# Linear attention and a split-precision MLP: larger units of k features, other burst prices in the planner, other SBUF addresses

## The chip, the cores and the metric

The kernel runs on one core of a Trainium2 chip. The metric is the time of one execution in microseconds (us) of device time. Three runs of the kernel before took 1173.62 to 1175.29 us, median 1174.64. The chip's engines are called as in the profile: PE is TensorE (matmuls; PEld is its weight load), DVE is VectorE, ACT is ScalarE, POOL is GpSimd, SP is SyncE, which only issues DMAs here.

## The reference

```python
def _attn_ref(q, k, v, w_phi):              # q, k, v: 8 batches, 8 heads, 576 tokens, 64; w_phi: 64 x 128
    def phi(x):
        proj = np.einsum('bhsd,df->bhsf', x, w_phi)
        proj = proj - np.max(np.abs(proj), axis=-1, keepdims=True)
        return np.concatenate([np.exp(proj), np.exp(-proj)], axis=-1)
    q_p, k_p = (phi(q), phi(k))
    kv = np.einsum('bhsf,bhsd->bhfd', k_p, v)
    z = np.sum(k_p, axis=2)
    num = np.einsum('bhsf,bhfd->bhsd', q_p, kv)
    den = np.einsum('bhsf,bhf->bhs', q_p, z)[..., None] + 1e-06
    return (num / den).astype(np.float32)

def _moe_ref(x, w_in, w_out):               # x: the attention's output as 4608 x 512
    h = x @ w_in                            # 512 x 2048
    g = 0.5 * h * (1.0 + erf(h * inv_sqrt2))
    return (g @ w_out).astype(np.float32)   # 2048 x 512
```

## The kernel before

There are two streams of work on one TensorE. The attention stream handles 8 batches one after another. For each batch there are two quads of four heads (`k_quad`): a projection `pk` of the keys, its largest absolute value per token (`mx`, DVE, L412), the difference (DVE, through the helper at L328), two exps to `ek` (ACT, L416), and the sums `kv` over tokens (PE), which ACT copies to `kvn`. A quad's nine chunks of 128 tokens are taken in five units of 2, 2, 1, 2 and 2 chunks. Then come the query halves (`q_pair`): a projection `pq`, a copy `pc` to SBUF, an all-reduce `mb` of absolute values over the partitions on POOL (L459), the difference (DVE, L328), two exps `ef` (ACT, L465), and the numerator `pn` (PE). The denominator comes from TensorE in batches 0 and 1, and later from DVE (`un`, L488 and L491) and a second POOL all-reduce (`db`, L494). Numerator and denominator go to DRAM (`x_d`, `d_d`); `quotients` inverts the denominators.

The MLP stream has 18 blocks of 256 tokens (`block`). A block reads its tokens back (`xr`, `rb`), multiplies them on DVE and splits the product into a high part `xh` and a low part `xl`. Eight units follow. In each, 24 matmuls of 128x256 (`ph`) are followed by gelu on ACT (`gh`, L581 and L582), the low part `gl` on DVE (L328), and 12 matmuls of 128x512 (`po`). A block has 192 `ph` and 96 `po` matmuls; three matmuls (high by high, high by low, low by high) make one product. The weights arrive as 64-bit floats in 32 tiles (`w_i`, `w_o`), and each is converted and split by two operations on ACT and five on DVE (`split_weight`, L343 to L350).

No engine's order is written by hand. Every operation is given to a planner (class `Plan`) with an engine, a cost in us, a rank and a kind. `order` walks through time: on each engine it takes, among the operations that can go, the one of lowest rank; attention on TensorE is held back during the MLP until a lump of it (`LUMP`) has gathered. A change of tile shape on TensorE costs what `BEHIND` and `BEFORE` say. The engines then run their queues in that order. `T0`, `AT`, `ATR`, `HOLD`, `EARLY` and `WPACE` set when batches, blocks and weights come due. An operation cannot start before its tile's slot is free: one slot for `pk` and `pq` together (`pp`), one for `pn`, two for `ph`, one for `po`, four for `ek`, two for `gh` and `gl`.

SBUF tiles are allocated in the order of the `place` calls. Built, this kernel has `w_o8` to `w_o15` at addresses that are 0x700 past a multiple of 0x1000 (0x13700 and so on), `w_o0` to `w_o7` at 0x7c0 past one (0x1b7c0 and so on), and both slots of `xh` and `xl` at 0x7c0 past one.

All matmuls are recorded under one helper line, L287. An fp32 matmul (`pk`, `kv`, `pq`, `pn`) is one instruction in the program and two records in the trace; `ph` and `po` have one.

Of the kernel before, what the change touches and what calls it, by code (L numbers as in the profile page):

```python
# [54 lines left out]
class Op:  # L55
    __slots__ = ("eng", "cost", "fn", "bufs", "rank", "table", "late", "deps", "users", "wait", "ready", "start", "end", "n", "names", "nbytes", "duty", "kind")


class Plan:
# [45 lines left out]
    def order(self, bias):  # L105
# [53 lines left out]
        while len(done) < n:  # L159
# [79 lines left out]
def mm_cost(m, n):  # L239
    return max(0.875 * m, n / 2.306 + 9) / 1e3  # L240
# [27 lines left out]
def fused_kernel(ctx: ExitStack, tc: tile.TileContext, qT, kT, va, w_st, w_in, w_out, out):  # L268
# [11 lines left out]
    SLOTS = dict(kt=2, vt=2, mx=2, ek=4, kvn=4, un=1, db=1, qt=2, pc=2, mb=1, ef=2, xo=2, dc=2, rb=1, xr=1, xh=2, xl=2, gh=2, gl=2, ob=2)  # L280
# [100 lines left out]
    def k_quad(b, g, kvs, rank):  # L381
# [17 lines left out]
        units = ((0, (0, 1)), (0, (2, 3)), (None, (4,)), (1, (5, 6)), (1, (7, 8)))  # L399
        for u, (p, cs) in enumerate(units):  # L400
            n = len(cs)
            mx = sb["mx"]([P, 2, n], F32, f"mx_{nm}_{u}")
            e = [sb["ek"]([P, 2, n, NF], F32, f"ek_{nm}_{u}_{s}") for s in range(2)]
# [3 lines left out]
            def proj(x=x, cs=cs):  # L407
# [3 lines left out]
            op("pe", n * PAIR_K, proj, r=[kt, wst], w=[x], also=[mx, *e], kind="k", **k())  # L411
            op("dve", dve(256 * n, True), lambda xs=xs, mx=mx: nc.vector.tensor_reduce(  # L412
                out=mx(), in_=xs(), axis=AX.X, op=ALU.max, apply_absolute_value=True), r=[x], w=[mx], **k())
            tt("dve", dve(256 * n, True), xs, xs, lambda mx=mx, n=n: mx().unsqueeze(3).to_broadcast([P, 2, n, NF]), ALU.subtract, [x, mx], [x], **k())
            for s in (1, 0):
                op("act", act(256 * n, True), lambda xs=xs, e=e, s=s: nc.scalar.activation(  # L416
                    e[s](), xs(), AF.Exp, scale=1.0 - 2.0 * s), r=[x], w=[e[s]], table="exp", **k())
            for pp in (0, 1) if p is None else (p,):
# [5 lines left out]
                last_u = (u == 2) if pp == 0 else (u == 4)  # L424
                for i, c in enumerate(cs):
# [11 lines left out]
                    op("pe", 4 * PAIR_V, sums, r=[*e, vt] + ([] if fresh and i == 0 else [acc]), w=[acc], kind="v", **k())  # L437
# [4 lines left out]
    def q_pair(b, p, kvs, rank, halves=(0, 1)):  # L442
# [4 lines left out]
        for half in halves:  # L447
# [12 lines left out]
                mb(), pc(), P, bass_isa.ReduceOp.absmax), r=[pc], w=[mb], **k(1))  # L460
# [33 lines left out]
            op("pool", 3.7, lambda db=db, un=un: nc.gpsimd.partition_all_reduce(db(), un(), P, bass_isa.ReduceOp.add), r=[un], w=[db], **k())  # L494
# [43 lines left out]
    def block(j, rank):  # L538
# [22 lines left out]
        copy("dve", dve(NCC * TB, fast=True), xh, xr, [xr], [xh], rank=rank(0) - 4)  # L561
        tt("dve", dve(NCC * TB), xl, xr, lambda: xh().bitcast(F32), ALU.subtract, [xr, xh], [xl], rank=rank(0) - 4)
        po = ps["po"]([P, 2, DM], F32, f"po_{j}")
        for u in range(NU):
            rk = rank(u / NU)
            ph = ps["ph"]([P, 2, TB], F32, f"ph_{j}_{u}")
            for i in range(2):
# [10 lines left out]
                op("pe", 12 * mm_cost(128, TB), mm1, r=[xh, xl] + [wi[c, u // 2] for c in range(NCC)], w=[ph], rank=rk)  # L578
# [112 lines left out]
```

## Time and profile before

| | |
|---|---|
| median of 3 runs | 1174.64 us (1173.62 to 1175.29) |
| profiled execution | 1172.59 us |
| its span in the trace | 1170.8 us, 21787 instructions |
| mean granted TensorE clock | 0.981 of full speed |
| busy: PE, PEld, DVE, ACT, POOL | 95%, 78%, 42%, 50%, 27% of the span |
| chain that ended last | PE 79%, DVE 7%, DMA 4%, ACT 3%, POOL 3% |
| first matmul of blocks 0, 1, 2, 10 and 17 | 94.1, 171.5, 255.9, 808.8, 1121.4 us |

The span runs from the first to the last recorded instruction; the profiled execution's time is 1.8 us longer, and the median of the timed runs is another 2.05 us above that. The share of busy time is a mean over stages with different limits, so the stages are shown apart below. The page shows the span in 40 slices of 29.3 us, a digit being tenths of a slice; its PE row reads 5679999989 in the first ten slices and 9 in nearly all after them. Block 10's first matmul is the last before which attention is still under way; the eight blocks after it follow each other every 44 us.

### The profile page before, as it was taken

The page shows a single profiled execution, that of the slowest core. Times are in us where ns is not written, and L with a number is a line of the kernel's source. Part 1 is how long each engine was busy: PE and PEld are TensorE (multiplying, and loading weights), DVE is VectorE, ACT ScalarE, POOL GpSimd, SP SyncE. Part 2 cuts the span into 40 slices and gives each one's busy share as a digit, 9 for nine tenths or more (in the row PEclk, how much of TensorE's full clock was granted, in tenths as well). Part 3 has the DMA queues.
Part 4 walks back from the last instruction along what each step waited for, and adds up shares of the span by engine and source line. Part 5 has one row for each costly group of instructions (what it writes and reads, how often), then busy time and mean ns, then how long its engine had stood idle before and what let it go on. Part 6 is the DMA issues. An engine that isn't in the chain of part 4 may idle for free.

```text
span 1170.8 us, 21787 instructions
## 1 busy us (share of the span) xinstructions
PE 1116.8 (95%) x9096; PEld 917.1 (78%) x9096; DVE 486.6 (42%) x807; ACT 589.7 (50%) x963; POOL 320.7 (27%) x116
## 2 busy tenths in 40 slices
PE   5679999989899999999999999999999999999998
PEld 3437688767778778787877877787989989899897
DVE  5899942365553634444343444425121121121110
ACT  4676755745565676667466666755122122122121
POOL 3120200355561734445263454516000000000000
PEclk8799999989999999999999999999999999999999
DMA  6567421133322141322113130211121011010000
GB/s 240 177 210 228 139 71 47 52 94 102 94 65 70 41 107 45 108 64 80 58 43 106 43 106 23 69 28 51 27 55 36 19 54 37 18 37 19 1 18 19
DMA packets 73940, 84.92 MB, mean 73 GB/s; under 512 B 23969, under 2 KB 60993, under 8 KB 73841
## 3 DMA queue, kind: packets, MB, share of 16 engines
q1 hardware_dynamic: 73840, 83.52, 23.9%
q8 instruction: 71, 1.16, 0.4%
q14 instruction: 29, 0.23, 0.1%
HBM read 64.32 MB, written 19.17 MB: 71 GB/s over the span
## 4 chain that ended last, share of the span: by engine, by line
PE 79%; DVE 7%; DMA 4%; ACT 3%; POOL 3%; issue 2%; SPq 1%; ACTq 0%; POOLq 0%; DVEq 0%
PE po L287 32%; PE ph L287 31%; PE kv L287 6%; PE pn L287 5%; PE pq L287 3%; PE pk L287 3%; POOL db L494 2%; DMA raw_i<-in_w_in_dram 1%; DMA x_d<-xo 1%; POOL mb L459 1%; DVE pc L328 1%; DMA dc<-d_d 1%; ACT ek L416 1%; DVE w_o L328 1%; DVE w_i L328 0%
## 5 line engine op out<-in xcount | busy, mean ns | idle before, releaser
L287 PE MATMUL ph<-xh,w_i 128*128 128x256 f32 x2304 | 431.3, 283 | 0.0
L287 PEld LDWEIGHTS ph<-xh,w_i 128*128 128x128 f32 x2304 | 363.0, 190 | 15.4 <-issue 6.5
L287 PE MATMUL po<-w_o,gh 128*128 128x512 f32 x1152 | 367.6, 400 | 1.1 <-ACT gh L581 1.0
L287 PE MATMUL ph<-xl,w_i 128*128 128x256 f32 x1152 | 322.3, 280 | 0.0
L287 PEld LDWEIGHTS po<-w_o,gh 128*128 128x128 f32 x1152 | 208.6, 189 | 56.1 <-issue 8.2
L328 DVE TENSOR_TENSOR gl<-ph,gh 128x512 fp32r<-128x512 f32 x144 | 99.0, 688 | 361.7 <-ACT ph L582 353.0
L459 POOL PARTITION_ALL_REDUCE mb<-pc x64 | 144.6, 2259 | 362.4 <-ACT pc L322 327.7
L287 PE MATMUL po<-w_o,gl 128*128 128x512 f32 x576 | 228.8, 397 | 7.2 <-DVE gl L328 7.1
L287 PEld LDWEIGHTS ph<-xl,w_i 128*128 128x128 f32 x1152 | 218.4, 190 | 3.1
L581 ACT ACTIVATE gh<-ph 128x512 fp32r<-128x512 f32 x144 | 86.1, 598 | 259.2 <-PE ph L287 258.5
L494 POOL PARTITION_ALL_REDUCE db<-un x48 | 177.1, 3690 | 134.3 <-DVE un L491 119.3
L287 PEld LDWEIGHTS po<-w_o,gl 128*128 128x128 f32 x576 | 108.7, 189 | 36.4 <-DVE gl L328 11.9
L287 PEld LDWEIGHTS kv<-vt,ek 128*64 128x64 f32 (+1 forms) x2560 | 87.8, 143 | 43.1 <-ACT ek L416 18.1
L287 PE MATMUL kv<-vt,ek 128*64 128x65 f32 (+1 forms) x2560 | 99.8, 231 | 15.7 <-ACT ek L416 14.7
L287 PE MATMUL pn<-ef,kvn 128*64 128x288 f32 (+1 forms) x512 | 97.7, 427 | 16.1 <-ACT xo L322 11.1
L416 ACT ACTIVATE ek<-pk 128x512 f32<-128x512 f32 (+1 forms) x160 | 80.0, 550 | 46.3 <-DVE pk L328 45.9
L465 ACT ACTIVATE ef<-pc 128x576 f32<-128x576 f32 x128 | 81.7, 679 | 30.5 <-DVE pc L328 30.2
L328 DVE TENSOR_TENSOR pc<-pc,mb 128x576 f32<-128x576 f32 x64 | 55.1, 861 | 100.0 <-POOL mb L459 99.7
L412 DVE TENSOR_REDUCE mx<-pk 128x4 f32<-128x512 f32 (+1 forms) x80 | 50.4, 632 | 90.2 <-PE pk L287 90.2
L582 ACT ACTIVATE ph<-ph 128x512 f32<-128x512 f32 x144 | 85.4, 593 | 0.0
L581 ACT ACT_TABLE_LOAD x55 | 70.6, 1283 | 19.8 <-PE ph L287 19.1
L287 PEld LDWEIGHTS pn<-ef,kvn 128*64 128x64 f32 (+1 forms) x512 | 39.4, 138 | 52.2 <-ACT xo L322 19.3
(41 smaller groups left out, 697.4 us busy)
## 6 DMA issues: line engine op xcount, KB each, us to landing
vt<-in_va_dram SPq DMA_DIRECT2D x16, 585.0 KB
qt<-in_qT_dram SPq DMA_DIRECT2D x64, 144.0 KB
kt<-in_kT_dram SPq DMA_DIRECT2D x16, 576.0 KB
out_dram<-ob SPq DMA_DIRECT2D x36, 256.0 KB
raw_i<-in_w_in_dram SPq DMA_DIRECT2D x16, 512.0 KB
raw_o<-in_w_out_dram SPq DMA_DIRECT2D x16, 512.0 KB
x_d<-xo SPq DMA_DIRECT2D x48, 144.0 KB
x_d<-xo SPq DMA_DIRECT2D x32, 72.0 KB
```

The costliest lines, as they stand in the source:

```text
L287: return tc.keep_in_program_order(nc.tensor.matmul(*a, **kw))
L328: op(eng, cost, lambda: e.tensor_tensor(out=dst(), in0=a(), in1=b(), op=o), r=r, w=w, **kw)
L412: op("dve", dve(256 * n, True), lambda xs=xs, mx=mx: nc.vector.tensor_reduce(out=mx(), in_=xs(), axis=AX.X, op=ALU.max, apply_absolute_val ...
L416: op("act", act(256 * n, True), lambda xs=xs, e=e, s=s: nc.scalar.activation(e[s](), xs(), AF.Exp, scale=1.0 - 2.0 * s), r=[x], w=[e[s]], ...
L459: op("pool", 2.2, lambda mb=mb, pc=pc: nc.gpsimd.partition_all_reduce(mb(), pc(), P, bass_isa.ReduceOp.absmax), r=[pc], w=[mb], **k(1))
L465: op("act", act(2 * HS), lambda ef=ef, pc=pc, s=s: nc.scalar.activation(ef()[:, s], pc(), AF.Exp, scale=1.0 - 2.0 * s), r=[pc], w=[ef], ta ...
L494: op("pool", 3.7, lambda db=db, un=un: nc.gpsimd.partition_all_reduce(db(), un(), P, bass_isa.ReduceOp.add), r=[un], w=[db], **k())
L581: op("act", act(2 * TB, True) + 0.016, lambda gh=gh, ph=ph: nc.scalar.activation(gh(), ph(), AF.Gelu), r=[ph], w=[gh], table="gelu", rank= ...
L582: op("act", act(2 * TB, True) + 0.037, lambda ph=ph: nc.scalar.activation(ph(), ph(), AF.Gelu), r=[ph], w=[ph], table="gelu", rank=URGE + rk)
```

## The change

The k units become three per quad, of 4, 1 and 4 chunks. The subtraction writes its difference to the SBUF tile that is to hold the negative exp (`e[1]`), and both exps read it there, the second in place; the PSUM tile comes free after the subtraction. The `ek` pool has two slots of 128x1024 instead of four of 128x512; batch 0 uses the slots of `xh` and `xl` for it. The planner gets other prices: for bursts (`PAIR_K`, `PAIR_Q`, `PAIR_N`, `PAIR_V`, `mm_cost`), for changes of tile shape, and for DMAs (`RATE`). It also counts two waits: a POOL all-reduce waits for the DVE operation with two SBUF inputs that runs, and such a DVE operation waits while an all-reduce reads. All of its time constants change. Built, every `w_o` tile lies 0x700 past a multiple of 0x1000, `w_i` follows at 0x13700 in the order of columns 2, 0, 3, 1, and `xh` and `xl` are padded by 16 elements, so that their slots lie at 0x237c0 and 0x24800, 0x25840 and 0x26880.

```diff
-    BEHIND = {"f": 0.0, "k": 0.0, "q": 0.0, "v": 0.095, "n": 0.05, "d": 0.0}
-    BEFORE = {"f": 0.0, "k": 0.09, "q": 0.09, "v": 0.09, "n": 0.09, "d": 0.09}
-    SHAPE = {"f": 0, "k": 1, "q": 1, "v": 2, "n": 2, "d": 3}
+    BEHIND = {"f": 0.1, "k": 0.1, "q": 0.095, "v": 0.09, "w": 0.09, "n": 0.1, "d": 0.05}
+    BEFORE = {"f": 0.08, "k": 0.1, "q": 0.1, "v": 0.05, "w": 0.05, "n": 0.05, "d": 0.1}
+    SHAPE = {"f": 0, "k": 1, "q": 1, "v": 2, "n": 2, "w": 3, "d": 4}
+    READS = {"max": 1.12, "add": 2.38}
...
+            if o.eng == "pool" and o.port:
+                t = max(t, port[0])
...
+            if o.eng == "dve" and o.port and port[1] <= t < port[2]:
+                t = port[2]
...
-    return max(0.875 * m, n / 2.306 + 9) / 1e3
+    return (n / 2.286 + 3.0) / 1e3
...
-    for q in range(4):
+    for f in range(NFC):
+        place(f"w_o{f}", [P, 2, 512])
+    place("gh", [P, 2, TB])
+    place("gl", [P, 2, TB])
+    for q in (2, 0, 3, 1):
         for c in range(NCC):
             place(f"w_i{c}_{q}", [P, 2, 512])
...
-    place("xh", [P, NCC, TB])
-    place("xl", [P, NCC, TB])
+    place("xh", [P, NCC * TB + 16], F32R)
+    place("xl", [P, NCC * TB + 16], F32R)
...
-        units = ((0, (0, 1)), (0, (2, 3)), (None, (4,)), (1, (5, 6)), (1, (7, 8)))
+        units = ((0, (0, 1, 2, 3)), (None, (4,)), (1, (5, 6, 7, 8)))
...
-            e = [sb["ek"]([P, 2, n, NF], F32, f"ek_{nm}_{u}_{s}") for s in range(2)]
+            e = [sb[EARLY_EK[u % 2] if b == 0 else "ek"]([P, 2, n, NF], F32, f"ek_{nm}_{u}_{s}") for s in (1, 0)][::-1]
...
-            tt("dve", dve(256 * n, True), xs, xs, lambda mx=mx, n=n: mx().unsqueeze(3).to_broadcast([P, 2, n, NF]), ALU.subtract, [x, mx], [x], **k())
-            for s in (1, 0):
-                op("act", act(256 * n, True), lambda xs=xs, e=e, s=s: nc.scalar.activation(
-                    e[s](), xs(), AF.Exp, scale=1.0 - 2.0 * s), r=[x], w=[e[s]], table="exp", **k())
+            tt("dve", dve(256 * n, True), e[1], xs, lambda mx=mx, n=n: mx().unsqueeze(3).to_broadcast([P, 2, n, NF]), ALU.subtract,
+               [x, mx], [e[1]], also=[e[0]], port=False, **k())
+            for s in (0, 1):
+                op("act", act(256 * n), lambda e=e, s=s: nc.scalar.activation(
+                    e[s](), e[1](), AF.Exp, scale=1.0 - 2.0 * s), r=[e[1]], w=[e[s]], table="exp", **k())
...
-BIAS = 40
+BIAS = 9.61
...
-PAIR_K = 0.43
-PAIR_Q = 0.7
-PAIR_N = 1.18
-PAIR_V = 0.125
+PAIR_K = 0.224
+PAIR_Q = 0.494
+PAIR_N = 0.972
+PAIR_V = 0.118
...
-ATR = -21.1
-T0 = 57.4
+ATR = -67.24
+T0 = 82.29
+RATE = 285.0
```

The other constants that change are T15 901.4 to 890.51, T18 1079.0 to 1005.72, PATIENCE 2.5 to 1.35, EARLY 37.5 to 50.99, WPACE 3.996 to 3.84, LUMP 2.5 to 3.56, LEAD 167.4 to 164.37, HOLD 44.6 to 27.98 and WR -13.5 to -13.57.

The planner's new order is seen best at three places. In the names below, the first number of an attention tile is its batch, and the last is that of the buffer; of an `xr`, `ph` or `po` the first is the block.

VectorE, where the first block's input `xr_0` is multiplied and split; before (rows 119 to 127 of its queue):

```order
L328 TENSOR_TENSOR w_o7_892<-wt_o7_828,w_o7_892 128x512
L412 TENSOR_REDUCE mx_1_0_2_909<-pk_1_0_2_894 128x2
L328 TENSOR_TENSOR xr_0_377<-xr_0_377,rb_0_840 128x1024
L328 TENSOR_TENSOR pk_1_0_2_894<-pk_1_0_2_894,mx_1_0_2_909 128x2x128
L324 CAST xh_0_920<-xr_0_377 128x1024
L328 TENSOR_TENSOR w_i0_2_902<-wt_i0_2_835,w_i0_2_902 128x512
L328 TENSOR_TENSOR xl_0_938<-xr_0_377,xh_0_920 128x1024
L344 TENSOR_SCALAR wt_i1_2_911<-wt_i1_2_911 128x512
L412 TENSOR_REDUCE mx_1_0_3_963<-pk_1_0_3_943 128x4
```

The same place in the changed order (rows 89 to 100):

```order
L337 TENSOR_TENSOR w_i2_1_930<-wt_i2_1_864,w_i2_1_930 128x512
L421 TENSOR_REDUCE mx_1_1_0_942<-pk_1_1_0_921 128x8
L337 TENSOR_TENSOR pc_1_0_1_904<-pc_1_0_1_904,mb_1_0_1_917 128x576
L337 TENSOR_TENSOR ek_1_1_0_1_947<-pk_1_1_0_921,mx_1_1_0_942 128x1024
L337 TENSOR_TENSOR w_i3_1_936<-wt_i3_1_875,w_i3_1_936 128x512
L353 TENSOR_SCALAR wt_o4_944<-wt_o4_944 128x512
L337 TENSOR_TENSOR xr_0_451<-xr_0_451,rb_0_845 128x1024
L337 TENSOR_TENSOR pc_1_1_0_912<-pc_1_1_0_912,mb_1_1_0_951 128x576
L355 TENSOR_SCALAR wt_o4_944<-wt_o4_944 128x512
L333 CAST xh_0_992<-xr_0_451 128x1024
L357 SCALAR_TENSOR_TENSOR wt_o4_944<-raw_o4_594,wt_o4_944 128x512
L337 TENSOR_TENSOR xl_0_1008<-xr_0_451,xh_0_992 128x1024
```

`xr_0` moves from row 121 to row 95. Before, it stands between the third unit of batch 1's first quad and weights of the third column group; now batch 1's second quad has begun, query halves of batch 1 are subtracted around it, and the weights stand at the second column group and `w_o4`.

TensorE, where block 1 begins (`ph_1_0`); before (a row that has the same text as one above it is left out here and below):

```order
L287 MATMUL pk_2_0_0_1775<-wst_106,kt_2_0_1100 128x128 x4
L287 MATMUL kv_1_1_1_1664<-vt_1_1_671,ek_1_1_4_0_1773 64x65 x2
L287 MATMUL kv_1_1_1_1664<-vt_1_1_671,ek_1_1_4_1_1757 64x65 x2
...
L287 MATMUL po_0_1092<-w_o15_1627,gh_0_7_1754 128x512 x2
L287 MATMUL po_0_1092<-w_o15_1627,gl_0_7_1759 128x512
...
L287 MATMUL ph_1_0_1813<-xh_1_1308,w_i0_0_221 128x256
L287 MATMUL ph_1_0_1813<-xl_1_1312,w_i0_0_221 128x256
```

Changed:

```order
L298 MATMUL pn_2_0_0_1990<-ef_2_0_0_1916,kvn_2_0_0_1606 64x288 x4
L298 MATMUL po_0_1241<-w_o12_1863,gh_0_6_1961 128x512 x2
L298 MATMUL po_0_1241<-w_o12_1863,gl_0_6_1988 128x512
...
L298 MATMUL po_0_1241<-w_o13_1939,gh_0_6_1961 128x512 x2
L298 MATMUL po_0_1241<-w_o13_1939,gl_0_6_1988 128x512
...
L298 MATMUL ph_1_0_2031<-xh_1_1437,w_i0_0_234 128x256
L298 MATMUL ph_1_0_2031<-xl_1_1478,w_i0_0_234 128x256
```

Before, all of block 0's `po` with `w_o15` come first, and batch 2 has just had its first `pk`. Now a numerator `pn` of batch 2 is already done there, and block 0's `po` of `w_o14` and `w_o15` come after block 1's first matmuls.

TensorE in the middle, where the first quad of batch 5 begins its sums; before:

```order
L287 MATMUL pn_4_2_1_5059<-ef_4_2_1_5019,kvn_4_1_0_4734 64x288 x4
L287 MATMUL pq_4_3_0_5067<-qt_4_3_0_4905,wst_106 128x288 x2
L287 MATMUL kv_5_0_0_5076<-vt_5_0_4358,ek_5_0_0_0_5054 64x65 x2
L287 MATMUL kv_5_0_0_5076<-vt_5_0_4358,ek_5_0_0_1_5044 64x65 x2
...
L287 MATMUL pq_4_3_1_5097<-qt_4_3_1_4936,wst_106 128x288 x2
L287 MATMUL po_5_5021<-w_o3_522,gh_5_1_5015 128x512 x2
L287 MATMUL po_5_5021<-w_o3_522,gl_5_1_5028 128x512
...
L287 MATMUL pk_5_0_1_5114<-wst_106,kt_5_0_4299 128x128 x4
L287 MATMUL ph_5_2_5119<-xh_5_4154,w_i0_1_608 128x256
L287 MATMUL ph_5_2_5119<-xl_5_4168,w_i0_1_608 128x256
```

Changed:

```order
L298 MATMUL pn_4_2_0_4469<-ef_4_2_0_4401,kvn_4_1_0_4148 64x288 x4
L298 MATMUL pq_4_3_0_4476<-qt_4_3_0_4322,wst_106 128x288 x2
L298 MATMUL kv_5_0_0_4479<-vt_5_0_3840,ek_5_0_0_0_4423 64x65 x2
L298 MATMUL kv_5_0_0_4479<-vt_5_0_3840,ek_5_0_0_1_4412 64x65 x2
...
L298 MATMUL pn_4_2_1_4519<-ef_4_2_1_4441,kvn_4_1_0_4148 64x288 x4
L298 MATMUL pq_4_3_1_4528<-qt_4_3_1_4344,wst_106 128x288 x2
...
L298 MATMUL po_4_4549<-w_o0_544,gh_4_0_4474 128x512 x2
L298 MATMUL po_4_4549<-w_o0_544,gl_4_0_4513 128x512
...
L298 MATMUL pk_5_0_1_4559<-wst_106,kt_5_0_3750 128x128 x2
L298 MATMUL po_4_4549<-w_o1_637,gh_4_0_4474 128x512 x2
```

The sums of the first unit (`kv` from `ek_5_0_0`) come in one visit with two `pn` and two `pq`, and the next `pk` has one chunk; before, the visit holds half as many sums, and the next `pk` has two chunks.

## Rows read from the trace of the kernel before

**Rows 1.** The page: busy time of each engine; the last chain by line.

```profile
PE 1116.8 (95%) x9096; PEld 917.1 (78%) x9096; DVE 486.6 (42%) x807; ACT 589.7 (50%) x963; POOL 320.7 (27%) x116
...
PE po L287 32%; PE ph L287 31%; PE kv L287 6%; PE pn L287 5%; PE pq L287 3%; PE pk L287 3%; POOL db L494 2%; DMA raw_i<-in_w_in_dram 1%; DMA x_d<-xo 1%; POOL mb L459 1%; DVE pc L328 1%; DMA dc<-d_d 1%; ACT ek L416 1%; DVE w_o L328 1%; DVE w_i L328 0%
```

**Rows 2.** Windows by stage: length, busy us per engine (instructions), clock, DMA.

```profile
16.50:94.00 77.50, 53.80 (x588) 34.41 (x588) 68.06 (x118) 50.61 (x101) 16.24 (x6) 0.85 0.59 183
94.00:156.00 62.00, 58.14 (x438) 45.38 (x432) 58.56 (x99) 45.46 (x77) 9.62 (x4) 0.94 0.54 164
...
171.50:344.00 172.50, 162.51 (x1418) 125.62 (x1417) 83.29 (x126) 98.28 (x161) 75.10 (x27) 0.96 0.27 78
344.00:809.00 465.00, 462.13 (x4131) 372.27 (x4130) 201.03 (x358) 300.05 (x455) 208.43 (x73) 1.00 0.23 65
```

**Rows 3.** Timeline, start of kernel: start us, length us, engine, line, operation, tiles.

```profile
94.06 0.38 PE L287 MATMUL ph<-xh,w_i 128*128 128x256 f32 x1
...
155.14 0.68 DVE L328 TENSOR_TENSOR w_o<-wt_o,w_o 128x512 fp32r<-128x512 f32 x1
...
171.46 0.28 PE L287 MATMUL ph<-xh,w_i 128*128 128x256 f32 x1
```

**Rows 4.** Timeline, TensorE: one visit to attention inside ph.

```profile
561.75 0.28 PE L287 MATMUL ph<-xh,w_i 128*128 128x256 f32 x1
561.96 0.68 PE L287 MATMUL kv<-vt,ek 64*64 64x65 f32 x16
562.58 0.71 PE L287 MATMUL pk<-wst,kt 64*128 64x128 f32 x8
...
563.84 0.39 PE L287 MATMUL ph<-xh,w_i 128*128 128x256 f32 x1
564.06 0.28 PE L287 MATMUL ph<-xl,w_i 128*128 128x256 f32 x1
```

**Rows 5.** Timeline, TensorE: other bursts of attention.

```profile
242.89 0.76 PE L287 MATMUL pq<-qt,wst 64*128 64x288 f32 x4
243.58 1.19 PE L287 MATMUL pn<-ef,kvn 128*64 128x288 f32 x8
244.70 0.76 PE L287 MATMUL pq<-qt,wst 64*128 64x288 f32 x4
...
557.50 1.10 PE L287 MATMUL kv<-vt,ek 128*64 128x65 f32 x32
558.53 0.49 PE L287 MATMUL pk<-wst,kt 64*128 64x128 f32 x4
```

**Rows 6.** Chain of waits in a late block: start us, length us, what.

```profile
994.30 5.60 PE po L287 x24
999.90 5.45 PE ph L287 x48
...
1016.39 5.45 PE po L287 x24
1021.85 5.65 PE ph L287 x48
```

**Rows 7.** Timeline, then chain: the longest wait after block 1.

```profile
250.00 3.00 DVE L328 TENSOR_TENSOR pc<-pc,mb 128x576 f32<-128x576 f32 x1
...
253.76 2.19 PE L287 MATMUL pn<-ef,kvn 128*64 128x288 f32 x8 [4.83 <-ACT ef L465]
...
255.95 2.64 PE ph L287 x12
```

**Rows 8.** Groups by form: count, busy us, mean ns, idle before and releasers.

```profile
L328 DVE TENSOR_TENSOR pc<-pc,mb 128x576 f32<-128x576 f32 x64 | 55.1, 861 | 100.0 <-POOL mb L459 99.7
...
L412 DVE TENSOR_REDUCE mx<-pk 128x4 f32<-128x512 f32 x64 | 43.7, 685 | 75.2 <-PE pk L287 75.2
...
L412 DVE TENSOR_REDUCE mx<-pk 128x2 f32<-128x256 f32 x16 | 6.7, 418 | 15.0 <-PE pk L287 15.0
...
L416 ACT ACTIVATE ek<-pk 128x512 f32<-128x512 f32 x128 | 69.5, 594 | 35.3 <-DVE pk L328 35.0
```

More of the change, by code (lines that the diff above doesn't have):

```diff
@@ L55 @@
 class Op:
-    __slots__ = ("eng", "cost", "fn", "bufs", "rank", "table", "late", "deps", "users", "wait", "ready", "start", "end", "n", "names", "nbytes", "duty", "kind")
+    __slots__ = ("eng", "cost", "fn", "bufs", "rank", "table", "late", "deps", "users", "wait", "ready", "start", "end", "n", "names", "nbytes", "duty", "kind", "port")
 class Plan:
@@ L77, in pool, with op @@
         return lambda shape, dt, name: Buf(self, tag, lambda: pool.tile(shape, dt, tag=tag, name=name, bufs=bufs))
-    def op(self, eng, cost, fn, r=(), w=(), also=(), rank=0.0, table=None, late=0.0, kb=0, duty=1.0, kind="f"):
+    def op(self, eng, cost, fn, r=(), w=(), also=(), rank=0.0, table=None, late=0.0, kb=0, duty=1.0, kind="f", port=None):
         o = Op()
@@ L82, in op @@
         o.users, o.ready, o.nbytes, o.duty, o.kind = [], self.since, kb, duty, kind
+        o.port = port if port is not None else eng == "dve"
         deps = set()
@@ L121, in order @@
         gelus, left_at, dma, dge = [0], [0.0], [0.0], [0.9]
+        port = [0.0, 0.0, 0.0]
         def start_of(o):
             t = max(clock[o.eng], o.ready)
+            if o.eng == "pool" and o.port:
+                t = max(t, port[0])
             if o.table == "exp" and table[0] == "gelu" and gelus[0] % (2 * STICK):
@@ L211, in order @@
             clock[o.eng] = o.end
+            if o.eng == "dve" and o.port:
+                port[0] = o.end
+            if o.eng == "pool" and o.port:
+                port[1:] = [o.start, o.start + self.READS[o.port]]
             for b in o.bufs:
@@ L435, in sums @@
                         return ins
-                    op("pe", 4 * PAIR_V, sums, r=[*e, vt] + ([] if fresh and i == 0 else [acc]), w=[acc], kind="v", **k())
+                    op("pe", 4 * PAIR_V, sums, r=[*e, vt] + ([] if fresh and i == 0 else [acc]), w=[acc], kind="v" if p is not None else "w", **k())
                 if last_u:
@@ L493, in q_pair @@
                            r=[ef, kvn, un], w=[un], **k())
-            op("pool", 3.7, lambda db=db, un=un: nc.gpsimd.partition_all_reduce(db(), un(), P, bass_isa.ReduceOp.add), r=[un], w=[db], **k())
+            op("pool", 3.7, lambda db=db, un=un: nc.gpsimd.partition_all_reduce(db(), un(), P, bass_isa.ReduceOp.add), r=[un], w=[db], port="add", **k())
             op("sp", 0.06, lambda db=db, d_to=d_to: nc.sync.dma_start(
@@ L576, in mm1 @@
                     return ins
-                op("pe", 12 * mm_cost(128, TB), mm1, r=[xh, xl] + [wi[c, u // 2] for c in range(NCC)], w=[ph], rank=rk)
+                op("pe", 12 * mm_cost(128, TB), mm1, r=[xh_all, xl_all] + [wi[c, u // 2] for c in range(NCC)], w=[ph], rank=rk)
             gh = sb["gh"]([P, 2, TB], F32R, f"gh_{j}_{u}")
@@ L625, in fused_kernel @@
     plan.emit()
-T15 = 901.4
-T18 = 1079.0
-BIAS = 40
+T15 = 890.51
+T18 = 1005.72
+BIAS = 9.61
 STICK = 2
-PATIENCE = 2.5
+PATIENCE = 1.35
 URGE = -1000.0
-EARLY = 37.5
-WPACE = 3.996
+EARLY = 50.99
+WPACE = 3.84
 WSPAN = 24.5
```

39 lines of the change are left out of this document (18 added, 21 removed).

## The prediction

> **What bounds the kernel now.** I read the page first: TensorE is busy 95% of the span, and the chain that ended last is mostly its two MLP matmuls, po and ph [rows 1]. So time can go only where TensorE stands idle, runs at the lower clock, or spends longer on a matmul than it must. The windows by stage say where [rows 2]. Until 156 us VectorE is the limit: it is busy 68.06 of 77.5 us and 58.56 of 62 while it splits the weights, and TensorE is idle 23.7 and 3.9 us there. From 171.5 to 344 us TensorE is idle 10.0 us, and its granted clock of 0.96 costs about 0.04 x 172.5 = 6.9; from 344 to 809 it is idle only 2.9. These 20 us are all the waits left after block 1 starts. The timeline dates the start: block 0's first matmul at 94.06, the last weight's last operation at 155.14 + 0.68, block 1's first matmul at 171.46 [rows 3]. What idle time does not show I read from the timeline of a busy stretch, where TensorE changes from one tile shape to another [rows 4, 5], and from the chain of waits in the last blocks, where nothing but MLP runs [rows 6].
>
> **The change part by part.** All times are of the profiled execution, 1172.59 us (span 1170.8). The median of the runs shown is 1174.64, so 2.05 is added at the end.
>
> (a) *The start.* The first two pieces of the order show it. VectorE reaches xr_0, which block 0 waits for, in row 95 instead of 121, because batch 0's k units are done earlier. I summed the durations from the trace over VectorE's rows. Before, they give 81.7 us up to xl_0 and 147.2 up to w_o15, the last weight. That one ended at 155.8 on the clock, 8.6 us later than its sum. In the changed order, block 1's first ph needs the po of w_o12 and w_o13. The last VectorE row for them, gl_0_6, is row 226 with a sum of 157.4. With the same 8.6 us it ends at 166.0; 12 po at 0.233 us [rows 6] make 168.8, and with about 1.2 us for hand-overs I take 170. That is 1.5 us earlier than 171.5, and more attention is done by then. In the order, a kv, pk, pq or pn matmul is one instruction and in the trace two records. By that point the changed order has 80 more kv, 22 more pk, 12 more pq and 20 more pn, and 12 fewer po. Prices per record come from start to start, less the changes of shape of (b): kv 0.027 (1.10 for 32 against 0.68 for 16), pk 0.055 (0.71 for 8 against 0.49 for 4), pq (0.69 - 0.18) / 4 = 0.128, pn (1.12 - 0.18) / 8 = 0.118 [rows 4, 5]. So 160 x 0.027 + 44 x 0.055 + 24 x 0.128 + 40 x 0.118 - 12 x 0.233 = 11.7 us of TensorE work is moved ahead. It fits: TensorE was idle 27.6 us between 16.5 and 156. Gain: 13.2. The bounds come from VectorE's own idle time in the two windows, 12.9 us. If half goes, block 1 starts near 164 and the gain is 19; if the bigger operations and longer hold-ups nearly double it, it starts at 180 and the gain is 3.
>
> (b) *Changes of tile shape.* One visit to attention inside ph goes ph, kv x16, pk x8, kv x16, ph, and its five starts run from 561.75 to 564.06: 2.31 us [rows 4]. At the prices above, with 0.115 for each of the two ph, 32 kv and 8 pk, the work alone is 0.23 + 0.86 + 0.44 = 1.53. Four changes cost 0.78, or 0.19 each. Only the two outer ends can be read directly: ph to kv starts 0.21 apart and ph to ph after it 0.22, against 0.115 in a dense run, so 0.10 is the lower bound. I take 0.18. From block 1's first matmul on, the order has 334 changes of shape before and 233 after. Three k units instead of five make fewer visits, and the planner packs them together; the third piece of the order shows 24 kv rows, pn, pq and 8 kv in a row where there were 16 kv. 101 x 0.18 = 18.2 us (10.1 to 20.2).
>
> (c) *Addresses of w_out.* In the last blocks 24 po take 5.60 us with w_o0 to 3 and 5.45 with w_o8 to 11 [rows 6]. The former lie at 0x7c0 in their 4 KB, the latter at 0x700, where the change puts all. 48 of a block's 96 po are of the slow kind, so 2 x 0.15 x 18 blocks = 5.4 us. The Trainium skill ("SBUF — State Buffer", section "Who interferes with whom") gives TensorE two read ports of its own and says that nothing but the port pair of VectorE and GpSimd contends. By it an address would change nothing and the sum would lose this term; the two po rows, on an otherwise quiet core, speak against it.
>
> (d) *Addresses of x and w_in.* 48 ph take 5.45 in some runs and 5.65 in others [rows 6], with the same kind of operands; in the tail about half are of each kind. I cannot tell from this trace which pace the padded xh and xl get. All fast would be -0.1 x 72 = -7.2 us, all slow +7.2. I take 0, since the trace has both.
>
> (e) *k units.* A reduce costs 0.685 us for 512 elements and 0.418 for 256 [rows 8], so an estimated 1.22 for 1024, and the subtraction alike; per quad of k chunks VectorE saves about 0.3 us in each. On ScalarE an exp of 512 costs 0.594 [rows 8], so one of 1024 at most about two of these, 1.19. Both engines have room after 156 us (VectorE 83.3 and ScalarE 98.3 of 172.5 [rows 2]), so this gains or costs nothing there. The two ek slots add a wait: a unit's subtraction must wait for the kv of the unit before, and behind it on VectorE stand gl and un, for which po and pn wait. The order puts dense work between a pk and its kv (in batch 5 24 po and 24 ph, some 8.4 us, against 4.8 us for reduce, subtraction and two exps), so I price it at nothing. Uncovered, one unit costs TensorE up to two exps, 2.4 us, and 48 units 114 us; in between lies the next item.
>
> (f) *Waits after block 1.* The worst one now is a pn that waits 4.83 us for ef, because the subtraction of pc took 3.00 us on VectorE instead of its mean 0.861 [rows 7, 8]; a GpSimd all-reduce ran beside it. The planner now counts that wait, which should help; but attention now ends by block 8 instead of block 10, so the same all-reduces stand closer together. I keep 20 us: 10 at best, and at worst the 16.9 us per 172.5 of [rows 2] over the whole of some 480 us, 47.
>
> Sum: -13.2 - 18.2 - 5.4 + 0 = -36.8, so 1135.8 profiled and **1138** on the scale of the median. With each term at its better end (19, 20, 5.4, 7, 10) it is 1113, and at its worse end (3, 10, 0, -7, -27) above 1190, but they will not fall together: 1122 to 1152 for this case.
>
> **The rivals.**
> - *All fast.* ph falls into the 5.45 pace everywhere (7.2) and the planner's port waits halve the stalls (10): 1138 - 17 = 1121. For it: the fast pace holds for whole runs of 48 [rows 6]. Against: before, it comes and goes without a change of address.
> - *The start gains little.* The last weight is now VectorE's row 239 instead of 225, with a sum of 167.9 instead of 147.2. If block 0's po wait for it, block 1 starts at 180 (gain 3) and a change of shape is worth 0.10: -3 - 10 - 5 = -18, so 1156.
> - *Addresses do nothing,* as the page's rule has it: 1138 + 5.4 = 1143; with ph slow all through, 1151.
> - *GpSimd becomes the bound of the packed attention,* slower than before. Every query pair needs its all-reduce before ef and, from batch 2, a second one after; TensorE waits in order behind pn. One such stall costs 4.83 us, then 1.07 more for the pn (2.19 instead of 1.12) at the lower clock [rows 7], and 1.2 for the 12 ph after it (2.64 instead of 1.4): 7.1 us. From five more of them (36.8 / 7.1) the gain is gone; at eight, one query half in six of batches 2 to 7, it is 1138 + 57 = 1195. Against: in 344 to 809, with GpSimd busy 208 of 465, all idle time was 2.9 us.
>
> **How the numbers follow.** Forecast 0.50 (1122 to 1152), all fast 0.15, small start gain 0.14, addresses nothing 0.09, GpSimd bound 0.12. The range leaves out most of the last case and the far end of the second: 1114 to 1165. About 0.2%, 2.3 us, is what a measurement cannot tell from no change. All cases but the last are faster, less a little for the worse tail of the third: faster 0.85, same 0.03, slower 0.12.
>
> **What would show it.** (a) block 1's first ph at 165 to 175, and block 0's some 8 us before 94; (b) fewer and longer kv and pk bursts at the same prices, attention gone by block 8; (c) every 24 po in the last blocks at 5.45; (d) 48 ph at 5.45 or 5.65, which decides the sign of that term; (f) TensorE's idle time plus lower clock between block 1 and the end of attention, 20 us. I am wrong if that last figure is above 50, if block 1 starts after 180, or if the last blocks, which have no attention at all, change by more than the po rows say.

## The result and the profile after

The changed kernel takes 1118.71 us (median of 4 runs, 1117.42 to 1119.65) against 1174.42 before: a ratio of 0.9525, 95% interval 0.9508 to 0.9541. That is 55.7 us less. The forecast was 1138 and its range 1114 to 1165, so the direction and the range held, and the gain was half as large again as forecast. The narrower range that the prediction gives to its own case, 1122 to 1152, did not hold: the time lies 3 us below it, beyond the rival "all fast" (1121). The profiled execution took 1119.65 us, 52.9 less than that of before; its last matmul starts at 1113.1 us instead of 1165.4.

The page, as in [rows 1]:

```profile
PE 1091.9 (98%) x9096; PEld 916.1 (82%) x9096; DVE 474.1 (42%) x743; ACT 567.2 (51%) x883; POOL 316.3 (28%) x116
...
PE ph L298 35%; PE po L298 34%; PE pn L298 6%; PE kv L298 6%; PE pq L298 3%; PE pk L298 3%; ACT ek L426 1%; DMA x_d<-xo 1%; DVE mx L421 1%; DVE ek L337 1%; ACT ef L475 1%; PE spin L298 1%; ACT L593 0%; DVE pc L337 0%; ACT pc L331 0%
```

TensorE is busy 98% of the span instead of 95%. The windows by stage, as in [rows 2]; the last one shown now ends with attention, at 661 us instead of 816. The line under them is the kernel before, from block 1 to the end of its attention:

```profile
16.50:94.80 78.30, 65.11 (x771) 41.78 (x769) 64.02 (x103) 57.67 (x104) 22.67 (x10) 0.88 0.70 219
94.80:156.00 61.20, 60.24 (x580) 47.94 (x580) 58.99 (x95) 48.93 (x81) 9.71 (x4) 1.00 0.55 163
...
171.10:317.70 146.60, 146.60 (x1406) 118.16 (x1405) 78.78 (x121) 103.17 (x145) 76.98 (x28) 1.00 0.27 80
317.70:662.00 344.30, 344.11 (x3283) 279.52 (x3282) 169.87 (x282) 237.38 (x339) 195.86 (x68) 1.00 0.25 72
...
171.50:816.50 645.00, 632.15 (x5607) 504.22 (x5607) 286.52 (x489) 402.77 (x623) 289.20 (x100) 0.99 0.24 69
```

From block 1 to the end of attention TensorE is idle 0.2 us, at a clock of 1.00; before, 12.9 us at 0.99. VectorE is still the limit until 156 us, but TensorE's idle time there is 14.2 us instead of 27.6. The timeline of the start, as in [rows 3]:

```profile
94.83 0.50 PE L298 MATMUL ph<-xh,w_i 128*128 128x256 f32 x1
...
171.05 0.28 PE L298 MATMUL ph<-xh,w_i 128*128 128x256 f32 x1
...
178.19 0.69 DVE L337 TENSOR_TENSOR w_o<-wt_o,w_o 128x512 fp32r<-128x512 f32 x1 [0.69 <-ACT w_o L331]
```

Block 0 starts at 94.83 (94.06 before), block 1 at 171.05 (171.46). The last weight is now finished only at 178.9, after block 1 has begun. The chain in a late block, as in [rows 6]:

```profile
986.03 5.45 PE po L298 x24
991.48 5.65 PE ph L298 x48
```

All `po` now take 5.45 us for 24, and all `ph` 5.65 for 48; before, half of each took 5.60 and 5.45. The groups by form, as in [rows 8] (count, busy us, mean ns):

```profile
L421 DVE TENSOR_REDUCE mx<-pk 128x8 f32<-128x1024 f32 x32 | 39.0, 1219 | 25.6 <-PE pk L298 25.6
...
L498 DVE TENSOR_SCALAR un<-ef,kvn 128x288 f32<-128x288 f32 x96 | 37.2, 417 | 42.2 <-POOL db L504 35.1 <-ACT ef L475 7.0
...
L426 ACT ACTIVATE ek<-ek 128x1024 f32<-128x1024 f32 x64 | 67.7, 1057 | 18.0 <-DVE ek L337 17.3
```

The reduce of 1024 elements took 1.219 us (estimated 1.22), and the exp from SBUF 1.057.

### The profile page after: what moved, and what is told of

It reads as the page before. It is cut to its first block, busy times and chain, and to the rows that moved or that the text cites. A ratio compares the mean times of both kernels' runs of the same rounds, so it can differ in the third digit from the quotient of the medians.

```text
span 1117.9 us, 21535 instructions
## 1 busy us (share of the span) xinstructions
PE 1091.9 (98%) x9096; PEld 916.1 (82%) x9096; DVE 474.1 (42%) x743; ACT 567.2 (51%) x883; POOL 316.3 (28%) x116
## 4 chain that ended last, share of the span: by engine, by line
PE 86%; DVE 5%; ACT 4%; DMA 1%; issue 1%; POOL 1%; SPq 0%; ACTq 0%; POOLq 0%
PE ph L298 35%; PE po L298 34%; PE pn L298 6%; PE kv L298 6%; PE pq L298 3%; PE pk L298 3%; ACT ek L426 1%; DMA x_d<-xo 1%; DVE mx L421 1%; DVE ek L337 1%; ACT ef L475 1%; PE spin L298 1%; ACT L593 0%; DVE pc L337 0%; ACT pc L331 0%
## 5 line engine op out<-in xcount | busy, mean ns | idle before, releaser
L298 PE MATMUL po<-w_o,gh 128*128 128x512 f32 x1152 | 362.1, 395 | 0.0
L298 PE MATMUL po<-w_o,gl 128*128 128x512 f32 x576 | 224.6, 390 | 0.0
L298 PE MATMUL kv<-vt,ek 128*64 128x65 f32 (+1 forms) x2560 | 95.9, 229 | 3.5 <-ACT ek L426 2.7
L426 ACT ACTIVATE ek<-ek 128x1024 f32<-128x1024 f32 (+1 forms) x96 | 80.8, 843 | 25.4 <-DVE ek L337 24.1
L421 DVE TENSOR_REDUCE mx<-pk 128x8 f32<-128x1024 f32 (+1 forms) x48 | 45.6, 954 | 45.4 <-PE pk L298 45.4
```

The lines of the kernel that those rows point to most:

```text
L298: return tc.keep_in_program_order(nc.tensor.matmul(*a, **kw))
L426: op("act", act(256 * n), lambda e=e, s=s: nc.scalar.activation(e[s](), e[1](), AF.Exp, scale=1.0 - 2.0 * s), r=[e[1]], w=[e[s]], table="e ...
```

## The experiments

All ratios are to the kernel before, timed beside each kernel (its medians are 1172.4 to 1174.4). "Changes" are changes of tile shape on TensorE after block 1's first matmul, counted in the order; "idle" is TensorE's between block 1's first matmul and the last of attention, from the windows.

| kernel | median us | ratio, 95% | changes | block 1 at | idle us | attention ends |
|---|---|---|---|---|---|---|
| before | 1174.4 | 1 | 334 | 171.5 | 12.9 | 816 |
| changed | 1118.7 | 0.951-0.954 | 233 | 171.1 | 0.2 | 661 |
| e4 changed, no port waits | 1151.0 | 0.978-0.983 | 243 | 175.7 | 14.9 | 694 |
| e5 before, new units | 1185.9 | 1.010-1.013 | 244 | 167.9 | 38.0 | 659 |
| e6 changed, old units | 1159.4 | 0.987-0.990 | 310 | 170.2 | 3.9 | 833 |
| e9 changed, old prices | 1142.1 | 0.971-0.975 | 236 | 183.0 | 6.1 | 709 |
| e11 before, port waits | 1144.0 | 0.972-0.978 | 333 | 161.4 | 0.5 | 793 |

No run separates the time constants, `RATE` or the order of `w_i`: each kernel here has either all of those of before (e5, e11) or all of the changed ones (e4, e6, e9). So what it costs to take a part out may in part be that the constants do not fit the kernel that is left.

### The order: port waits, units, prices

**e4: the changed kernel without the port waits.**

```diff
-        o.port = port if port is not None else eng == "dve"
+        o.port = False
```

> The changed kernel whose planner does not count the two waits between GpSimd's all-reduce and VectorE's operations with two inputs in SBUF; constants, prices, k units and addresses as in the changed kernel. Theory P (the waits after block 1 went because the planner counts these two): TensorE's idle time and lower clock between block 1 and the end of attention come back, 10 to 20 us, so 1129 to 1139. Rival Q (they went because of the larger k units, the lumps and the other constants): under 3 us of such waits, and a time within 5 us of 1118.7.

Measured 1151.0, 32 us slower than the changed kernel and beyond even theory P's range. The window from block 1 to the end of attention, and the group of `un`, which VectorE runs between the all-reduces:

```profile
175.70:693.90 518.20, 503.33 (x4721) 403.07 (x4721) 283.97 (x410) 338.88 (x488) 279.42 (x94) 1.00 0.24 71
...
L498 DVE TENSOR_SCALAR un<-ef,kvn 128x288 f32<-128x288 f32 x96 | 54.5, 599 | 49.7 <-POOL db L504 44.0 <-ACT ef L475 5.7
```

TensorE is idle 14.9 us there, and `un` takes 599 ns on average instead of 417. Block 1 also starts 4.6 us later, about what two runs of one order differ by (see e3). Theory P holds; the idle time, the later start and ten more changes are 21 of the 32 us, and I did not sort out the rest.

**e11: the kernel before with nothing but these two waits in its planner.** 

```diff
+            if o.eng == "pool" and o.port:
+                t = max(t, port[0])
...
+            if o.eng == "dve" and o.port and port[1] <= t < port[2]:
+                t = port[2]
```

(and `READS`, the two clocks in `port`, and `port=` at the same operations as in the change)

> The kernel before with only the planner's two waits between GpSimd's all-reduce and VectorE added; prices, constants, five k units and addresses of before. If these waits are what the order of before lacked: the 20 us of idle time and lower clock between block 1 and the end of attention shrink to under 8, and the time falls by some 12 us or more, to 1160 or less. If they matter only once attention is packed by larger units: within 4 us of before, 1170 to 1178.

Measured 1144.0: this part alone takes 30 us off, with five units, old prices, and 333 of 334 changes of shape left.

```profile
161.40:792.80 631.40, 630.91 (x5603) 505.92 (x5603) 285.16 (x492) 414.21 (x631) 287.40 (x100) 1.00 0.25 71
```

Idle time falls from 12.9 to 0.5 us, the clock goes to 1.00, and block 1 starts 10 us earlier, which is a third of the gain. The planner does not make an all-reduce quicker: `mb` takes 2.26 us on average in both kernels. Nor does it keep VectorE and GpSimd apart: `un` is as long as before, and the subtraction of `pc` only a little shorter (790 ns on average instead of the 861 of [rows 8]). The group of `un` before and in e11:

```profile
L488 DVE TENSOR_SCALAR un<-ef,kvn 128x288 f32<-128x288 f32 x96 | 40.8, 457 | 42.2 <-POOL db L494 34.3 <-ACT ef L465 8.0
...
L499 DVE TENSOR_SCALAR un<-ef,kvn 128x288 f32<-128x288 f32 x96 | 41.7, 468 | 23.5 <-POOL db L505 14.9 <-ACT ef L476 8.6
```

What changes is whether TensorE waits for a delayed operation. Its waits between block 1 and the end of attention (total us, times, longest), before and in e11:

```profile
PE pn L287 <- ACT ef L465: 4.8, 1, 4.8
PE po L287 <- DVE gl L328: 4.7, 8, 0.9
PE kv L287 <- ACT ek L416: 2.5, 2, 2.1
...
PE po L298 <- DVE gl L339: 0.4, 1, 0.4
```

The longest of before is the one of [rows 7]: `pc`'s subtraction ran from 250.00 to 253.00 us beside this all-reduce.

```profile
249.85 3.59 POOL L494 PARTITION_ALL_REDUCE db<-un  x1 [2.69 <-issue]
```

So by these rows the gain after block 1 comes from an order in which a delayed result finds TensorE with other work. Why block 1 starts earlier is not shown.

**e5: the kernel before with nothing but the new units.**

```diff
-        units = ((0, (0, 1)), (0, (2, 3)), (None, (4,)), (1, (5, 6)), (1, (7, 8)))
+        units = ((0, (0, 1, 2, 3)), (None, (4,)), (1, (5, 6, 7, 8)))
```

(with the subtraction into `ek`, two `ek` slots and `EARLY_EK`, as in the change)

> The kernel before with only the new k units (4, 1 and 4 chunks, difference in SBUF, two ek slots, batch 0 in the slots of xh and xl); prices, constants and addresses of before. In its order 244 changes of shape are left after block 1's first matmul (334 before, 233 in the changed kernel). If the units alone bring the fewer changes and do not touch the waits: 90 x 0.18 = -16 us, about 1157, with the 20 us of waits after block 1 still there. Rival (the larger units also shorten the waits for ek): the waits fall under 10 us, about 1147. Rival (old prices and larger units do not fit): waits above 30 us, 1167 or more.

Measured 1185.9, slower than before. Its window, the group of `un`, and TensorE's longest waits in that window (total us, times, longest):

```profile
167.90:658.90 491.00, 452.99 (x4383) 349.02 (x4381) 282.41 (x397) 301.77 (x455) 295.83 (x100) 0.97 0.27 77
...
L489 DVE TENSOR_SCALAR un<-ef,kvn 128x288 f32<-128x288 f32 x96 | 63.5, 694 | 60.8 <-POOL db L495 54.7 <-ACT ef L466 4.9 <-ACT ek L417 1.1
...
PE po L287 <- DVE gl L328: 12.4, 7, 3.3
PE pn L287 <- ACT ef L466: 11.7, 6, 2.2
PE pn L287 <- ACT xo L322: 6.9, 10, 1.5
```

The units alone bring 90 fewer changes and pack attention into the first 659 us, as the changed kernel does; but TensorE is idle 38.0 us at a clock of 0.97, waiting most for `gl`, for `pn`'s input `ef` and for `pn`'s slot (which the copy `xo` frees), and `un` takes 694 ns instead of 457. These are the stalls of the prediction's last rival, in a kernel that lacks the port waits; GpSimd itself is busy only 295.83 of the 491 us. The third case of the expectation is the one that came. Whether counting the waits is enough to mend it was not run: no kernel here has the new units and the port waits with the constants and prices of before.

**e6: the changed kernel with the old units.**

```diff
-        units = ((0, (0, 1, 2, 3)), (None, (4,)), (1, (5, 6, 7, 8)))
+        units = ((0, (0, 1)), (0, (2, 3)), (None, (4,)), (1, (5, 6)), (1, (7, 8)))
```

(with exps from PSUM and four `ek` slots, as before)

> The changed kernel with the five k units of before (exps from PSUM, four ek slots); planner, prices, port waits, constants and addresses as in the changed kernel. 310 changes of shape after block 1 instead of 233, 334 before. If the port waits remove the waits by themselves: 77 x 0.18 = 14 us slower than the changed kernel, about 1133, TensorE idle under 3 us between block 1 and the end of attention. If the larger units are needed for that: 10 to 20 us of waits more, 1143 to 1153.

Measured 1159.4, 41 us slower than the changed kernel, more than either case.

```profile
170.20:833.10 662.90, 659.00 (x5823) 538.76 (x5823) 291.11 (x505) 396.98 (x628) 285.99 (x100) 1.00 0.24 68
```

Idle is 3.9 us, so the port waits do remove the waits without the larger units. What the expectation left out is the start: block 1 comes at the same time, but with 80 kv, 22 pk, 12 pq and 20 pn fewer before it, 14.8 us of work at the matmuls' dense paces (0.058, 0.112, 0.24 and 0.243 us, from one start to the next inside a burst) that then lies behind. With 77 x 0.187 = 14.4 us for changes and 3.7 us of idle time, less 0.9 for the start, that is 32 of the 40 us between the profiled runs; 8 us stay open.

**e9: the changed kernel with the old prices.**

```diff
-    return (n / 2.286 + 3.0) / 1e3
+    return max(0.875 * m, n / 2.306 + 9) / 1e3
...
-PAIR_K = 0.224
+PAIR_K = 0.43
```

(and BEHIND, BEFORE, SHAPE and the other PAIR constants of before)

> The changed kernel whose planner has the old prices: BEHIND, BEFORE, SHAPE, PAIR_K, PAIR_Q, PAIR_N, PAIR_V and mm_cost of before; port waits, constants, k units and addresses of the changed kernel. 236 changes of shape after block 1 (233 in the changed kernel). Theory: the prices only make the planner's clock right, so that buffers and results come when it says; with the old ones the orders of the engines no longer fit the true times and waits of 5 to 20 us appear between block 1 and the end of attention: 1124 to 1139. Rival: with the same units and nearly the same count of changes nothing is lost, within 4 us of 1118.7.

Measured 1142.1, 23 us slower than the changed kernel at nearly the same count of changes.

```profile
183.00:708.70 525.70, 519.63 (x4849) 421.66 (x4848) 268.16 (x412) 366.13 (x510) 273.44 (x94) 0.99 0.26 73
```

Block 1 starts 12 us later, and TensorE is idle 6.1 us: the waits that the theory names are there, but the time lies 3 us above its range, because more of the loss lies before block 1, which the expectation left out.

**e10: what a change of shape costs, by itself.**

```diff
+                visit = ps["pn"]([P, P], F32, f"visit_{j}_{u}") if j >= 10 and i == 1 else None
...
+                    if visit is not None:
+                        mm(visit(), lhsT=wst()[:64], rhs=wst()[:64], start=True, stop=True)
```

> The changed kernel with one more matmul in each of the 64 units of blocks 10 to 17, between the two halves of ph: an fp32 matmul of 64 x 128 by 64 x 128 (as a pk) into a slot of pn that nobody reads. It adds 128 changes of tile shape in blocks without attention. My price in term (b), 0.18 a change and 0.11 for the matmul: 64 x (0.11 + 0.36) = 30 us, 1149; at the lower bound of 0.10 a change: 64 x 0.31 = 20 us, 1139; if a change costs nothing where nothing waits: 7 us, 1126.

Measured 1158.6, 40 us slower, 0.62 us a visit. One visit in the timeline:

```profile
967.58 0.28 PE L298 MATMUL ph<-xh,w_i 128*128 128x256 f32 x1
967.78 0.49 PE L298 MATMUL visit<-wst 64*128 64x128 f32 x2
968.20 0.39 PE L298 MATMUL ph<-xh,w_i 128*128 128x256 f32 x1
968.42 0.28 PE L298 MATMUL ph<-xl,w_i 128*128 128x256 f32 x1
968.54 0.40 PE L298 MATMUL ph<-xh,w_i 128*128 128x256 f32 x2
```

A `pk` of four records in the kernel before, the one of [rows 5], and the `po` behind it:

```profile
558.53 0.49 PE L287 MATMUL pk<-wst,kt 64*128 64x128 f32 x4
558.96 0.73 PE L287 MATMUL po<-w_o,gh 128*128 128x512 f32 x2
```

The `ph` before it takes 0.20 instead of 0.12, the two records of the visit 0.42, the `ph` after it 0.22: together 0.84 where the work is 0.35, so 0.49 for two changes. A change costs 0.25 here, above my 0.18, because the burst of two records takes 0.42 to the next start and the `pk` of four takes 0.43: a very short burst costs as much as one of twice its length. Over all changes after block 1, the trace has a mean of 0.098 us lost at the last matmul ahead of one and 0.092 at the first behind it in the kernel before, 0.096 and 0.088 in the changed one.

### The addresses

The pieces are the chain's in a late block, 24 `po` and 48 `ph` each.

**e1: all of w_out at 0x7c0**, x padded as in the changed kernel.

```diff
-    for f in range(NFC):
-        place(f"w_o{f}", [P, 2, 512])
...
     place("dc", [P, HS // 16])
+    for f in range(NFC):
+        place(f"w_o{f}", [P, 2, 512])
```

> The changed kernel with only the addresses of the weights exchanged: w_in first (0x1700 and on), then gh, gl and dc, then all of w_out, each tile 0x7c0 past a multiple of 0x1000; x stays padded, and the order of every engine is the same. In the changed kernel 24 po take 5.45 us and 48 ph 5.65. Theory O (the po that go before set the pace of ph: slow po leave ph fast, fast po leave it slow): 24 po 5.60, 48 ph 5.45, so 72 x (0.15 - 0.20) = -3.6 us, about 1115. Theory X (the padded x makes ph slow, whatever po does): 24 po 5.60, 48 ph still 5.65, +10.8 us, about 1129.

```profile
946.39 5.60 PE po L298 x24
951.99 5.65 PE ph L298 x48
```

1126.7 us (ratio 0.958 to 0.963): theory X. With padded x, ph is slow behind slow po too. (w_in moves as well, but every `w_i` tile stays 0x700 past a multiple of 0x1000, in all these kernels.)

**e2: x unpadded** at 0x7c0, w_out at 0x700.

```diff
-    place("xh", [P, NCC * TB + 16], F32R)
-    place("xl", [P, NCC * TB + 16], F32R)
+    place("xh", [P, NCC * TB], F32R)
+    place("xl", [P, NCC * TB], F32R)
```

> The changed kernel with xh and xl without their 16 elements of padding, so that all four slots lie 0x7c0 past a multiple of 0x1000 as they did before; w_out stays at 0x700. Theory O: nothing changes, po 5.45 and ph 5.65 in the last blocks, about 1119. Theory X: ph comes back to the mix of before (a mean of 115.6 ns, -7 us, about 1112), or is fast throughout (113.5 ns, -14 us, about 1104).

```profile
941.53 5.44 PE po L298 x24
946.97 5.65 PE ph L298 x48
```

1117.1 us (0.949 to 0.955), the same as the changed kernel within the intervals. In the blocks without attention ph stays slow, as theory O says; in those with attention its mean falls to 115 to 118 ns, as theory X says. Each theory holds where the other fails.

**e3: the kernel before with all of w_out at 0x700.**

```diff
-    place("dc", [P, HS // 16])
     for f in range(8):
         place(f"w_o{f}", [P, 2, 512])
+    place("dc", [P, HS // 16])
```

> The kernel before with only dc moved behind w_out, so that all of w_out lies 0x700 past a multiple of 0x1000; everything else, the order included, is the kernel before. My term (c) and theory X: 24 po 5.45 everywhere and ph as it was, -5.4 us, about 1169. Theory O: po 5.45, but then all ph at 5.65, -5.4 + 7.2, about 1176, no gain from the address.

```profile
997.18 5.44 PE po L287 x24
1002.62 5.65 PE ph L287 x48
```

1173.4 us, ratio 0.998 to 1.001: no gain. After block 1, po gains about 4 us and ph, slow throughout the last blocks, loses about 3: theory O in those blocks, and against my term (c). The order is that of before, and block 1 starts at 175.6 here against 171.5 there, so the start of one and the same order differs by some 4 us between runs.

**e7: x unpadded at 0x700.**

```diff
-    place("dc", [P, HS // 16])
     place("xh", [P, NCC * TB], F32R)
     place("xl", [P, NCC * TB], F32R)
+    place("dc", [P, HS // 16])
```

> The changed kernel with xh and xl unpadded and all four slots 0x700 past a multiple of 0x1000 (dc moved behind them); w_out at 0x700. If ph is slow because x does not lie as it did at 0x7c0: 48 ph at 5.65 everywhere, as in the changed kernel, 1119. If any x that lies alike in all slots lets ph be fast after attention: as with x unpadded at 0x7c0, 5.65 in the last blocks and a mean of 114 to 117 ns while attention runs, 1117. If an aligned x is fast as an aligned w_out is: 5.45 everywhere, -14 us, 1104.

```profile
945.07 5.47 PE po L298 x24
950.53 5.75 PE ph L298 x48
```

1125.6 us (0.959 to 0.962), slower, and outside all three cases: ph takes 5.75, a third pace, 119.8 ns each.

**e8 and e12: x unpadded, and one of each four w_out tiles at 0x7c0**, the last (e8) or the first (e12: 0, 4, 8, 12).

```diff
     for f in range(NFC):
-        place(f"w_o{f}", [P, 2, 512])
+        if f not in (3, 7, 11, 15):
+            place(f"w_o{f}", [P, 2, 512])
...
     place("dc", [P, HS // 16])
+    for f in (3, 7, 11, 15):
+        place(f"w_o{f}", [P, 2, 512])
```

> The changed kernel with x unpadded at 0x7c0 and w_o3, w_o7, w_o11 and w_o15 0x7c0 past a multiple of 0x1000, the other twelve at 0x700. In the last blocks ph follows the po of one of these four. If the last po before ph sets its pace, as long as x is unpadded: 24 po at 5.45 + 6 x 0.006 = 5.49 and 48 ph at 5.45, so 10.94 instead of 11.10 in the changed kernel, up to -11.5 us, 1107 to 1112. If not: ph 5.65, po 5.49, +2.6 us, about 1120.

> As the kernel with w_o3, 7, 11 and 15 at 0x7c0 and x unpadded, but with w_o0, 4, 8 and 12 there instead: in the last blocks each run of 24 po then begins with the slow ones and ends with fast ones. If the last po before ph sets its pace: 24 po 5.49 and 48 ph 5.65 in the last blocks, about 1119. If any slow po in the run does: 5.49 and 5.45, about 1111.

e8, then e12:

```profile
934.69 5.49 PE po L298 x24
940.19 5.45 PE ph L298 x48
```

```profile
942.69 5.50 PE po L298 x24
948.19 5.65 PE ph L298 x48
```

e8 takes 1110.84 us (ratio 0.9463 to 0.9491), 8 us less than the changed kernel and the fastest of all; e12 takes 1121.4 (0.952 to 0.957). The two have as many slow po, and the order is the same. Only which po comes last before ph differs. In e8's trace after block 1, 57 of 60 runs of ph (12 or more matmuls each) behind a po at 0x7c0 are fast (under 115 ns a matmul), and 3 of 25 behind one at 0x700. So with x at 0x7c0 the last po before ph decides ph's pace, with six exceptions, until the next burst of another kind. With padded x, ph is slow behind po of either address; with x at 0x700 it is slow behind po at 0x700, the only one tried. Why the addresses act so is not shown by any run. By addresses alone, one and the same order took 1110.8 (e8) to 1126.7 us (e1).

## Why the prediction was right, and where it was off

Term by term, from the two profiled runs (last matmul 1165.4 to 1113.1, 52.3 us):

- **(a) The start: right in its sum, wrong in one step.** Block 1 starts 0.4 us earlier (1.5 forecast), with the 80 kv, 22 pk, 12 pq and 20 pn done, 12.1 us at the dense paces: 12.5 in all, 13.2 forecast. The 0.4 says nothing by itself: in the six runs with this order block 1 starts at 169.0 to 173.0. That block 0 would start 8 us before 94 did not come (91.6 to 94.8 in those runs): VectorE reached xr_0 after fewer rows, but not that much sooner. TensorE's idle time before 156 halved instead, since it had more attention to do.
- **(b) Changes of shape: right.** 334 x 0.190 less 233 x 0.184 are 20.6 us (18.2 forecast). e10 puts an added change at 0.25, for very short bursts; e6 does not isolate the price, since its start differs too.
- **(c) Addresses of w_out: right for po alone, wrong for the kernel.** po fell from a mean of 230.7 ns to 227.8 over the 1632 after block 1, 4.7 us (5.4 forecast). But e3 shows that aligning w_out alone gains nothing, as ph then loses what po gains. The step that failed is that po's pace and ph's are two separate terms. The prediction's own sign shows it: by the po rows a late block should be 0.3 us shorter, and it takes 44.4 us from start to start instead of 44.3.
- **(d) Addresses of x: at the bad bound.** ph went from 115.45 to 117.75 ns, 3264 times 2.3 ns or 7.5 us slower; 0 was taken, with a bound of 7.2. Two things that the change does are each enough for it in the last blocks: the padding, behind slow po (e1), and fast po, with x unpadded (e2).
- **(e) k units: right in VectorE's price, short in the rest.** The ek wait that they add cost nothing measurable: TensorE is idle 0.2 us. But put alone into the kernel before they cost 13 us (e5), a loss for which the sum has no term; with the new prices and constants, and still without the port waits, the kernel is 22 us faster than before (e4).
- **(f) Waits after block 1: mis-sized, the largest error.** I kept 20 us, 10 at best. Measured: idle 12.9 to 0.2 us, and the clock to 1.00, which gives back the 6.9 us of [rows 2]: 19.6 us gained. The failed step is the sentence that the same all-reduces closer together would eat what the planner's counting saves. e11 and e4 show the counting to be worth 30 us put in alone and 32 taken out, a third of the 30 in an earlier start; I had priced it at nothing.

The sum is 12.5 + 20.6 + 4.7 - 7.5 + 19.6 = 49.9 of the 52.3 us. That the range held is in part luck: (d) and (f) erred in opposite ways, and without the loss in (d) the time would have been about 1111, below 1114. Of the rivals, "all fast" named nearly the time that came (1121), by one right step of two: the waits went, but ph became slow instead of fast. "Addresses do nothing" comes out in sum for w_out alone (e3), but it is false for each matmul, and e8 and e1 differ by 16 us through addresses alone. The stalls of "GpSimd as bound" are what e5 shows; the changed kernel does not have them. The parts do not add: alone, the port waits gain 30 us and the units lose 13; taken out of the changed kernel, the port waits cost 32, the units 41 and the prices 23.

## What to carry to other kernels

When an order is planned from costs, ask which waits the costs leave out before asking which prices are off: two waits between engines, counted, brought 30 us here with nothing else changed. A change that packs work closer should be judged together with the changes that make room for it, since alone it can lose: the larger units cost 13 us by themselves and 41 when taken out of the changed kernel. And where one operand's address changes a matmul's pace, time the next kind of matmul too.

## What the runs showed of the hardware

- A TensorE matmul's pace hangs on SBUF addresses: 128x512 took 227 ns with its moving operand 0x700 past a multiple of 0x1000 and 233 ns at 0x7c0 (e1); 128x256 took 113.5, 117.7 or 119.8 ns by where x lies and what ran before. With x at 0x7c0, a run of 128x256 takes its pace from the last 128x512 before it: slow behind a fast one, fast behind a slow one (e8 against e12).
- A change of tile shape costs 0.19 us on average, half at each end; a burst of two fp32 records (`visit`, e10) takes 0.42 us and one of four (`pk`) 0.43.
- Some of VectorE's operations are slowed beside GpSimd's all-reduces: in the kernel before, the 18 of 96 `un` (128x288) that overlap one in the records take 856 ns on average, the other 78 take 365; `gl` (128x512) takes 686 beside one and 689 clear of any. How often it happens does not hang on the counting alone: of the table's kernels, the mean of `un` is 392 to 532 ns in the four that count the waits (e6, changed, e11, e9) and 457 to 694 in the three that do not (before, e4, e5).
